# Retention scores of two heads: one full-height product on zero-padded queries, or two half-height products with a bank each

## The chip, the cores and the metric

The kernel runs on one core of a Trainium2 chip. A core has a matrix engine (TensorE, PE in the profile, with its weight loads shown apart as PEld), three engines for element-wise work (VectorE = DVE, ScalarE = ACT, GpSimd = POOL) and queues that start DMA transfers (SP among them). TensorE multiplies what lies in SBUF and writes the products to PSUM, which has eight banks of 128 rows x 512 float32 here; DVE and ACT read them from there. The metric is the device time of one execution in microseconds (us). The kernel before takes 247.51 us, the median of three runs (247.45 to 247.79).

## The reference, cut to what matters

Two layers follow each other. The first is a retention (a linear attention with decay), for 4 batches, 8 heads, 768 positions and 64 channels per head:

```python
gamma = 1.0 - 2.0 ** (-5.0 - np.arange(H))
for t in range(S):
    state = gamma * state + einsum('bhd,bhe->bhde', k[:, :, t], v[:, :, t])
    y[:, :, t] = scale * einsum('bhd,bhde->bhe', q[:, :, t], state)
```

The second layer takes the 8 x 64 channels of a position as one row of 512. It mixes the rows with the real part of a Fourier transform over positions and channels, adds that to the input (u), normalises u, and adds a two-layer network: `u + relu(norm(u) @ w_ch1) @ w_ch2`, with 2048 hidden channels.

## The kernel before, in words

**The retention in chunks.** The 768 positions are six chunks of 128 (NCH). Within a chunk the output is (scores x mask) x values; what came before the chunk enters through a 64 x 64 state per head. Two heads are worked on together, as the 64 + 64 rows of one 128-row tile. Four such pairs make a batch (PAIR_ORDER gives their order). For each pair of batches two to four (b = 1, 2, 3 in the code) these units are emitted:

- `cast_unit` brings q, k and v to 16 bits on POOL, with the decay of the keys folded in.
- `t_unit` transposes q and k, on TensorE for b = 1 (tiles `tq`, L550, copied out by ACT at L556 and L561) and by DMA for b = 2 and 3. The transposed keys `kT` hold head one in rows 0 to 63 and head two in rows 64 to 127. The transposed queries `qTz` exist twice: `qT[:, 0]` has head one in its upper rows and zeros below, `qT[:, 1]` zeros above and head two below.
- `a_unit` makes the scores. It has three parts of two chunks each. Because of the zeros, one product of all 128 rows with the 256 columns of both padded copies (L594) gives the scores of head one in the first 128 columns and of head two in the other 128. Two chunks fill one bank, `wkA`. One DVE instruction (L597) multiplies this bank of 512 columns by the causal mask with its decay, `maskp`, and writes `atm` in 16 bits.
- `kv_unit` makes the state: products `wkK` (L613), then a chain of DVE instructions (L623), with a copy by ACT (L619) at its head.
- `y_unit` makes the output: state products (L644), then the products of `atm` with the values (L648), in a bank per head, `wkY`. ACT evicts them (L656). It reads the padded queries too, in full height.

Batch one has units of its own (L458 for its scores, evicted at L465), in which the heads are taken from the half rows of an unpadded tile.

**The banks.** `wkA`, `wkK`, `wkY`, `tq` and the products of the Fourier part share the pool `ps_g` of five banks. The network's products `psh` and `psc` have the pool `ps_pm` of three.

**The network.** `h_unit` (L930) makes one block of 128 hidden channels by four products of 384 columns; ACT (L934) or DVE (L936) applies relu. `ch_unit` (L973) makes 128 output rows by sixteen products of 512 columns, in four units; DVE scales them and adds u (L977).

**The order.** The network of batch b and the retention and Fourier part of batch b + 1 run together. `attn_steps` makes six lists of units per batch (steps); each list, and the network's list, is a stream with a start and an end on a scale of batches. `emit` places the units of a stream evenly between these, merges all streams by place, and emits them in that order. For b = 2 and 3 the start and end of a step follow from the number of units in the steps. The framework then orders each engine's instructions. TensorE takes its instructions in order: when a product waits for a bank, all behind it wait. Loads of the batch after next wait for the last score product of pair 1 (`a_of`). `filler` (L145) are products on zeros that bridge idle time while batch one starts.

Of the kernel before, what the change touches and what calls it, by code (L numbers as in the profile page):

```python
# [12 lines left out]
ALU = mybir.AluOpType  # L13
f32 = mybir.dt.float32
# [4 lines left out]
P = 128  # L19
B, H, S, D = 4, 8, 768, 64  # L20
# [9 lines left out]
PAIR_ORDER = [0, 1, 3, 2]  # L30
# [7 lines left out]
def kernel(  # L38
# [9 lines left out]
    nc = tc.nc  # L48
# [3 lines left out]
    def pool(name, bufs, **kw):  # L52
        return ctx.enter_context(tc.tile_pool(name=name, bufs=bufs, **kw))
# [16 lines left out]
    ps_g = pool("ps_g", 5, space=PSUM)  # L70
# [13 lines left out]
    maskp = const.tile([P, NHP, 2, P], f32, tag="maskp")  # L84
# [36 lines left out]
    def held(unit):  # L121
        def run():
            ins = tc.nc.cur_bb.bb.instructions
            n0 = len(ins)
            unit()
            for n in range(n0, len(ins)):
                m = n - 1
                while m >= 0 and ins[m].engine != ins[n].engine:
                    m -= 1
                if m >= 0:  # L130
                    tc.add_manual_dep(ins[n], ins[m].name,
                                      mybir.DependencyInfo(mybir.DependencyClass.NoSync,
                                                           mybir.DependencyReason.DATA),
                                      reason="casts in turn")
        return run
# [450 lines left out]
    def a_unit(b, i, part):  # L586
        def run():
            st = at[b, i]
            if part == 0:
                st["atm"] = ap_.tile([P, NCH, 2, P], f16, tag="atm", name="atm")  # L590
            wk = ps_g.tile([P, 2, 2, P], f32, tag="g", name="wkA")
            for c2 in range(2):
                c = 2 * part + c2
                mm = nc.tensor.matmul(wk[:, c2], st["kT"][:, c, :], st["qT"][:, :, c, :],  # L594
                                      start=True, stop=True)
            a_of[b, i] = mm
            nc.vector.tensor_tensor(  # L597
                out=st["atm"][:, 2 * part:2 * part + 2], in0=wk,
                in1=maskp[:, PAIR_ORDER[i]].unsqueeze(1).to_broadcast([P, 2, 2, P]),
                op=ALU.mult)  # L600
        return run

    def kv_unit(b, i):
        def run():
            st = at[b, i]
            hp = PAIR_ORDER[i]
            kd, v16 = kd_of[b, i], v16_of[b, i]
            s16 = sp.tile([P, NCH - 1, P], f16, tag="s16", name="s16")
            st["s16"] = s16
            for c0, n in ((0, 3), (3, 2)):  # L610
                wk = ps_g.tile([P, 3, P], f32, tag="g", name="wkK", padded_shape=[P, 4, P])
                for c in range(c0, c0 + n):
                    nc.tensor.matmul(wk[:, c - c0, :], kd[:, c].rearrange("p a b -> p (a b)"),  # L613
                                     v16[:, c].rearrange("p a b -> p (a b)"),
                                     start=True, stop=True)
                for c in range(c0, c0 + n):
                    if c == 0:
                        if ON_ACT["kv"][min(b, 2)]:
                            nc.scalar.copy(s16[:, 0], wk[:, 0])  # L619
                        else:  # L620
                            nc.vector.tensor_copy(s16[:, 0], wk[:, 0])
                    else:
                        nc.vector.scalar_tensor_tensor(out=s16[:, c], in0=s16[:, c - 1],  # L623
                                                       scalar=gk2[:, hp:hp + 1],
                                                       in1=wk[:, c - c0],
                                                       op0=ALU.mult, op1=ALU.add)
        return run

    def y_unit(b, i):
        def run():  # L630
            st = at.pop((b, i))
            hp = PAIR_ORDER[i]
            v16, s16, atm, qT = v16_of[b, i], st["s16"], st["atm"], st["qT"]
            ypool, ytag = (ps_pm, "pm") if b == 0 else (ps_g, "g")
            yk = [ypool.tile([P, NCH, D], f32, tag=ytag, name="wkY", padded_shape=[P, 8, D])
                  for _ in range(2)]
            for c in range(1, NCH):
                for h2 in range(2):
                    sl = slice(64 * h2, 64 * h2 + 64)
                    if b == 0:  # L640
                        lhsT, rhs = qT[sl, c, :], s16[sl, c - 1, sl]
                    else:
                        lhsT, rhs = qT[:, h2, c, :], s16[:, c - 1, sl]
                    nc.tensor.matmul(yk[h2][:, c, :], lhsT, rhs,  # L644
                                     start=(c == 1), stop=False, skip_group_check=True)
            for h2 in range(2):
                for c in range(NCH):
                    nc.tensor.matmul(yk[h2][:, c, :], atm[:, c, h2, :], v16[:, c, h2, :],  # L648
                                     start=False, stop=(c == NCH - 1), skip_group_check=True)
                h = 2 * hp + h2  # L650
                x = xts[b % 2]
                if h < 4:
                    dst = x[:, :, 0, 64 * h + 1:64 * h + 65]
                else:
                    dst = x[:, :, 1, 513 - 64 * h:449 - 64 * h:-1]
                nc.scalar.activation(dst, yk[h2], AF.Copy, bias=0.0, scale=gq8[:, h:h + 1])  # L656
        return run
# [4 lines left out]
    def fold_s(b, lo, hi, s0, s1):  # L662
        def run():
            x = xts[b % 2]
            if b not in fd:
                fd[b] = dict(
                    ab=fp.tile([P, 2, 3, 2, XW], f16, tag="xab", name="xab"),
                    eo=fp.tile([P, 2, 2, 3, 256], f16, tag="eo", name="eo"),
                    g=gp.tile([P, 4, KN], f16, tag="g16", name="g16"),
                    gr=gp.tile([P, 4, 384], f16, tag="g16r", name="g16r"))  # L670
            ab = fd[b]["ab"]
            for a, op in ((0, ALU.add), (1, ALU.subtract)):
                nc.vector.tensor_tensor(out=ab[:, a, :, s0:s1, lo:hi],
                                        in0=x[:, 0:3, s0:s1, lo:hi],
                                        in1=x[:, 3:6, s0:s1, lo:hi], op=op)
        return run

    def fold_d(b, cb, es=(0, 1)):
        def run():
            ab, eo = fd[b]["ab"], fd[b]["eo"]  # L680
            i0 = 2 + 128 * cb
            for e in es:
                nc.vector.tensor_tensor(out=eo[:, e, :, :, 128 * cb:128 * cb + 128],
                                        in0=ab[:, :, :, 0, i0:i0 + 128],
                                        in1=ab[:, :, :, 1, i0:i0 + 128],
                                        op=(ALU.add, ALU.subtract)[e])
        return run
# [60 lines left out]
    def g0_unit(b, parts=(0, 1, 2)):  # L748
        def run():
            for part in parts:  # L750
                (g0_a, g0_b, g0_c)[part](b)
        return run
# [247 lines left out]
    def attn_steps(b):  # L1000
        steps = []
        for step in range(6):
            un = []
            if step < 4:
                un.append(held(cast_unit(b, step)))
            i = step - 1
            if 0 <= i < 4:
                un.append(kv_unit(b, i))
            i = step - 2
            if 0 <= i < 4:  # L1010
                un.append(y_unit(b, i))
                if i == 2:
                    un += [fold_s(b, 0, 130, 0, 2), fold_d(b, 0)]
                    if b < FB:
                        un += [g0_unit(b), s1_unit(b, 0, 0), s1_unit(b, 1, 0)]
            if step < 4:
                un.append(t_unit(b, step))
            i = step - 1
            if 0 <= i < 4:
                if b == 0:  # L1020
                    un += [a0_unit(b, i, 0), a0_unit(b, i, 1)]
                else:
                    un += [a_unit(b, i, part) for part in range(3)]
            if step == 5:
                un += [fold_s(b, 130, 258, 0, 2), fold_d(b, 1)]
                if b >= FB:
                    un += [g0_unit(b), fold_e(b, 0), fold_e(b, 1)]
            steps.append(un)
        return steps
# [148 lines left out]
```

## Time and profile before

| | |
|---|---|
| median time | 247.51 us |
| span of the profiled execution | 246.0 us |
| score products of batches two to four, L594 | 72, 128 x 256, first at 57.7 us, last at 175.2 us |
| their masked evictions, L597 | 36, 685 ns each, 23.9 us busy |
| score products of batch one, L458 | 48, half height, 128 columns |
| their evictions, L465 | 16, 548 ns each |
| network, L930 and L973 | 448 and 400 products |

How to read it: a busy time is the union of the engine's instructions; matmuls overlap each other, and an L594 product is shown with a length of 273 ns though the next one starts after 109 ns. So a cost on TensorE is read from the starts of neighbouring products. A chain lists the work that ended last, each piece released by the one ahead of it; an engine's idle time matters only where it is on this chain.

### The profile page before, as it was taken

The page shows a single profiled execution, that of the slowest core. Times are in us where ns is not written, and L with a number is a line of the kernel's source. Part 1 is how long each engine was busy: PE and PEld are TensorE (multiplying, and loading weights), DVE is VectorE, ACT ScalarE, POOL GpSimd, SP SyncE. Part 2 cuts the span into 40 slices and gives each one's busy share as a digit, 9 for nine tenths or more (in the row PEclk, how much of TensorE's full clock was granted, in tenths as well). Part 3 has the DMA queues.
Part 4 walks back from the last instruction along what each step waited for, and adds up shares of the span by engine and source line. Part 5 has one row for each costly group of instructions (what it writes and reads, how often), then busy time and mean ns, then how long its engine had stood idle before and what let it go on. Part 6 is the DMA issues. An engine that isn't in the chain of part 4 may idle for free.

```text
span 246.0 us, 5309 instructions
## 1 busy us (share of the span) xinstructions
PE 234.4 (95%) x2024; PEld 144.4 (59%) x2024; DVE 177.5 (72%) x430; ACT 124.3 (51%) x276; POOL 81.3 (33%) x146
## 2 busy tenths in 40 slices
PE   6897899999999999999999999999999998999994
PEld 2454668956676655665567446665666455445543
DVE  8998957898788788995987648887895657424122
ACT  8798669477785445742247415732257217202500
POOL 6667600376500068690001637660003214000000
PEclk9999999999999999999999999999999999999999
DMA  8998999699999287988999589596100331121012
GB/s 174 257 260 138 200 204 206 152 250 261 275 233 214 56 171 176 190 174 149 242 266 210 119 183 181 108 138 150 58 0 3 60 133 30 38 85 43 0 45 85
DMA packets 99209, 36.39 MB, mean 148 GB/s; under 512 B 89840, under 2 KB 96240, under 8 KB 99184
## 3 DMA queue, kind: packets, MB, share of 16 engines
q1 hardware_dynamic: 94960, 31.86, 62.5%
q0 software_dynamic: 4224, 4.19, 10.5%
q8 instruction: 16, 0.26, 0.5%
q14 instruction: 9, 0.07, 0.1%
HBM read 27.26 MB, written 6.29 MB: 136 GB/s over the span
## 4 chain that ended last, share of the span: by engine, by line
PE 72%; DVE 8%; POOL 7%; ACT 4%; SPq 3%; DMA 2%; issue 2%; POOLq 0%; DVEq 0%
PE psc L973 30%; PE psh L930 23%; SPq L159 3%; PE ps L730 3%; PE psh L947 3%; PE wkA L594 3%; DMA k<-in_k_dram 2%; PE wkY L648 2%; POOL u L864 2%; POOL u L866 2%; PE wkY L644 1%; DVE bst L883 1%; PE wkK L613 1%; DVE u L834 1%; PE pq L827 1%
## 5 line engine op out<-in xcount | busy, mean ns | idle before, releaser
L973 PE MATMUL psc<-w,ht 128*128 128x512 f16 (+1 forms) x400 | 89.6, 370 | 0.1
L930 PE MATMUL psh<-unT,w 128*128 128x384 f16 x448 | 81.3, 326 | 0.6 <-ACT ht L934 0.6
L973 PEld LDWEIGHTS <-ht 128*128 128x128 f16 x400 | 38.1, 98 | 35.5 <-issue 0.3
L930 PEld LDWEIGHTS <-w 128*128 128x128 f16 x448 | 42.3, 98 | 24.9 <-issue 1.3
L934 ACT ACTIVATE ht<-psh 128x384 f16<-128x384 f32 x64 | 30.6, 488 | 39.4 <-PE psh L930 38.3
L864 POOL TENSOR_TENSOR u<-u,x 128x256 f32<-128x256 f32 x21 | 13.3, 634 | 102.3 <-DVE u L834 90.7
L977 DVE SCALAR_TENSOR_TENSOR ob<-psc,stats,u 128x512 f32<-128x512 f32 (+1 forms) x25 | 18.1, 722 | 27.4 <-PE psc L973 27.3
L936 DVE TENSOR_SCALAR ht<-psh 128x384 f16<-128x384 f32 x48 | 26.3, 551 | 8.6 <-PE psh L930 8.3
L597 DVE TENSOR_TENSOR atm<-wkA,maskp 128x512 f16<-128x512 f32 x36 | 23.9, 685 | 1.0 <-PE wkA L594 1.0
L885 ACT ACTIVATE un<-u,stats 128x512 f16<-128x512 f32 x21 | 15.1, 721 | 16.9 <-DVE stats L884 8.7
L883 DVE BATCH_NORM_STATS2 bst<-u 128x6 f32<-128x512 f32 x21 | 14.6, 694 | 9.7 <-POOL u L866 9.5
L623 DVE SCALAR_TENSOR_TENSOR s<-s,gk,wkK 128x128 f16<-128x128 f16 x48 | 16.4, 343 | 2.3 <-ACT s L619 1.4
L656 ACT ACTIVATE x<-wkY,gexp 128x384 f16<-128x384 f32 x24 | 12.8, 580 | 9.3 <-PE wkY L648 9.3
L145 PE MATMUL wps<-ht 128*128 128x512 f16 x40 | 13.3, 439 | 2.2 <-POOL ht L196 2.2
L377 POOL TENSOR_SCALAR kd<-k,gexp 128x384 f16<-128x384 f32 x24 | 13.8, 584 | 2.4 <-DMA k<-in_k_dram 2.4
L866 POOL TENSOR_TENSOR u<-u,x 128x256 f32<-128x256 f32 x21 | 13.3, 634 | 2.8 <-DVE u L837 1.5
L594 PE MATMUL wkA<-qTz,kT 128*128 128x256 f16 x72 | 13.6, 273 | 0.0
L829 ACT COPY qn<-pq 128x128 f32<-128x128 f32 x18 | 4.9, 274 | 14.1 <-PE pq L827 13.9
L947 PE MATMUL psh<-unT,w 128*128 128x128 f16 x192 | 11.5, 219 | 0.1
L947 PEld LDWEIGHTS <-w 128*128 128x128 f16 x192 | 11.0, 98 | 0.7 <-issue 0.5
L382 POOL TENSOR_SCALAR v<-v 128x768 f16<-128x768 f32 x12 | 10.0, 830 | 2.0 <-DMA v<-in_v_dram 1.9
L594 PEld LDWEIGHTS <-kT 128*128 128x128 f16 x72 | 6.9, 98 | 6.0 <-DVE s L623 0.4
(164 smaller groups left out, 318.2 us busy)
## 6 DMA issues: line engine op xcount, KB each, us to landing
q<-in_q_dram SPq DMA_DIRECT2D x16, 384.0 KB, 6.2
k<-in_k_dram SPq DMA_DIRECT2D x16, 384.0 KB, 5.6
v<-in_v_dram SPq DMA_DIRECT2D x16, 384.0 KB, 6.6
out_dram<-ob SPq DMA_DIRECT2D x23, 256.0 KB, 2.6
w<-in_moe_w_ch_dram POOLq DMA_DIRECT2D x8, 512.0 KB, 11.1
out_dram<-ob SPq DMA_DIRECT2D x2, 128.0 KB, 1.7
unT<-un SPq DMA_TRANSPOSE x15, 2.4
qTz<-q16z SPq DMA_TRANSPOSE x8, 3.8
```

The lines of the kernel that those rows point to most:

```text
L594: mm = nc.tensor.matmul(wk[:, c2], st["kT"][:, c, :], st["qT"][:, :, c, :], start=True, stop=True)
L597: nc.vector.tensor_tensor(out=st["atm"][:, 2 * part:2 * part + 2], in0=wk, in1=maskp[:, PAIR_ORDER[i]].unsqueeze(1).to_broadcast([P, 2, 2, ...
L623: nc.vector.scalar_tensor_tensor(out=s16[:, c], in0=s16[:, c - 1], scalar=gk2[:, hp:hp + 1], in1=wk[:, c - c0], op0=ALU.mult, op1=ALU.add)
L864: nc.gpsimd.tensor_tensor(out=u[:, kb, 0:256], in0=u[:, kb, 0:256], in1=x[:, kb, 0, 1:257], op=ALU.add)
L866: nc.gpsimd.tensor_tensor(out=u[:, kb, 256:512], in0=u[:, kb, 256:512], in1=x[:, kb, 1, 257:1:-1], op=ALU.add)
L883: nc.vector.bn_stats(bst, u[:, kb, :])
L930: nc.tensor.matmul(psh, w116[:, cb, fb * P:(fb + 1) * P], unT[:, cb, rt * 384:(rt + 1) * 384], start=(cb == 0), stop=(cb == 3))
L934: nc.scalar.activation(ht16[:, fb, :], psh, AF.Relu, bias=0.0, scale=-1.0)
L936: nc.vector.tensor_scalar(out=ht16[:, fb, :], in0=psh, scalar1=-1.0, scalar2=0.0, op0=ALU.mult, op1=ALU.max)
L947: mm = nc.tensor.matmul(psh[:, f], w116[:, cb, fb * P:(fb + 1) * P], unT[:, cb, kb * P:(kb + 1) * P], start=(cb == 0), stop=(cb == 3))
L973: nc.tensor.matmul(psc[:, c0:c1], ht16[:, fb, rb3 * P:(rb3 + 1) * P], w216[:, fb, c0:c1], start=(fb == 0), stop=(fb == NFB - 1))
L977: nc.vector.scalar_tensor_tensor(out=ob[:, c0:c1], in0=psc[:, c0:c1], scalar=lb[b]["st"][:, rb, 3:4], in1=lb[b]["u"][:, rb, c0:c1], op0=AL ...
```

## The change

The scores of batches two to four are made as batch one makes them. `a_unit` gets two parts of three chunks in place of three of two. In each chunk, head one is a product of rows 0 to 63 of keys and queries alone, head two of rows 64 to 127. The heads write to a bank each (384 of its 512 columns). There are 144 products of 128 columns in place of 72 of 256, which do not multiply the zeros, and the two of a chunk stand in different row halves of the array. Each bank is evicted by its own DVE instruction of 384 columns, 48 in place of 36. The padded queries stay, since `y_unit` reads them. The aim is to use both halves of the array for two heads at once.

```diff
     def a_unit(b, i, part):
         def run():
             st = at[b, i]
+            hp = PAIR_ORDER[i]
             if part == 0:
                 st["atm"] = ap_.tile([P, NCH, 2, P], f16, tag="atm", name="atm")
-            wk = ps_g.tile([P, 2, 2, P], f32, tag="g", name="wkA")
-            for c2 in range(2):
-                c = 2 * part + c2
-                mm = nc.tensor.matmul(wk[:, c2], st["kT"][:, c, :], st["qT"][:, :, c, :],
-                                      start=True, stop=True)
+            wk = [ps_g.tile([P, 3, P], f32, tag="g", name="wkA", padded_shape=[P, 4, P])
+                  for _ in range(2)]
+            for c3 in range(3):
+                c = 3 * part + c3
+                for h2 in range(2):
+                    sl = slice(D * h2, D * h2 + D)
+                    mm = nc.tensor.matmul(wk[h2][:, c3, :], st["kT"][sl, c, :],
+                                          st["qT"][sl, h2, c, :], start=True, stop=True)
             a_of[b, i] = mm
-            nc.vector.tensor_tensor(
-                out=st["atm"][:, 2 * part:2 * part + 2], in0=wk,
-                in1=maskp[:, PAIR_ORDER[i]].unsqueeze(1).to_broadcast([P, 2, 2, P]),
-                op=ALU.mult)
+            for h2 in range(2):
+                nc.vector.tensor_tensor(
+                    out=st["atm"][:, 3 * part:3 * part + 3, h2, :], in0=wk[h2],
+                    in1=maskp[:, hp, h2].unsqueeze(1).to_broadcast([P, 3, P]), op=ALU.mult)
         return run
...
-                    un += [a_unit(b, i, part) for part in range(3)]
+                    un += [a_unit(b, i, part) for part in range(2)]
```

## The prediction

> **What bounds the kernel now.** I read three views: engine totals and the chain of the page, then a table by stretches, then the chain and the TensorE timeline around the products that change.
>
> ```profile
> PE 234.4 (95%) x2024; PEld 144.4 (59%) x2024; DVE 177.5 (72%) x430; ACT 124.3 (51%) x276; POOL 81.3 (33%) x146
> ...
> PE 72%; DVE 8%; POOL 7%; ACT 4%; SPq 3%; DMA 2%; issue 2%; POOLq 0%; DVEq 0%
> ```
>
> TensorE is busy for 95% and holds 72% of the chain that ended last. A matmul's end is modelled, though, so stretches are needed (columns: stretch, length, then busy us and instructions of PE, its weight loads, DVE, ACT, POOL).
>
> ```profile
> 57.00:80.00 23.00, 22.93 (x249) 15.63 (x247) 19.75 (x44) 16.38 (x31) 6.45 (x9) 1.00 1.19 243
> ...
> 100.00:126.00 26.00, 26.00 (x238) 16.33 (x237) 21.94 (x50) 10.77 (x25) 8.17 (x14) 1.00 1.08 194
> ...
> 150.00:178.00 28.00, 27.60 (x248) 17.14 (x247) 23.61 (x55) 11.65 (x28) 11.74 (x21) 1.00 0.63 130
> ```
>
> These are the stretches with the score products of batches two, three and four. PE has no gap in the middle one, 0.07 and 0.40 us in the others; DVE is at 84 to 86%. The chain there (start, length, engine, line):
>
> ```profile
> 106.76 0.22 PE wkA L594 x2
> 106.98 0.65 PE psh L930 x4
> 107.63 0.22 PE wkA L594 x2
> 107.85 0.65 PE psh L930 x4
> 108.50 0.22 PE wkA L594 x2
> 108.72 0.86 PE psc L973 x4
> ```
>
> The chain is TensorE's own queue, one product after another: 0.22 us for two score products, 0.109 each, with MLP products (psh, psc) on both sides. So any time that this queue gains or loses here reaches the end nearly one to one, and the question is what a group of half-height products costs *between full-height ones*. Batch one already does it (L458):
>
> ```profile
> 17.87 0.60 PE L145 MATMUL wps<-ht 128*128 128x512 f16 x2
> 18.41 0.51 PE L458 MATMUL wkA<-qTz,kT 64*128 64x128 f16 x12
> 18.85 0.39 PE L145 MATMUL wps<-ht 128*128 128x512 f16 x1
> ```
>
> Twelve half-height products, six pairs, start at 18.41; the next full-height one starts at 18.85. I also took the single starts from the trace. The two of a pair start 3 ns apart. Pair follows pair after 67, then 56, 56, 56, 56 ns. The last pair's second product is followed by the full-height one after 149 ns, not 53: 96 ns lost. The full 512-column product ahead of the group is followed by it after 312 ns, though such products otherwise follow each other after 216: again 96 ns. The first gap after the group is 226 ns, not 216. The entry into batch one's other half-height products (L520) is 126 against 29 ns behind 64-column products at 12.6 us, and 152 against 56 behind transposes at 23.1 us: 96 or 97 each time, whatever is ahead.
>
> **What the Trainium skill says.** *TensorEngine Tiling (Array Packing)*, Tiling Modes, Key Properties: "Changing tiling mode (not just tile) drains the TensorE". The trace agrees, with 96 ns on entry and 96 on exit. *TensorE: Matmul & The Clock Gate*, Part 3, The mechanism: products in different row groups overlap with about 4 ns between starts; here 3 to 4 ns. The tiling page, Gotcha 1: PSUM Pressure: different row tiles write to different banks; this is why each head now has a bank of its own. *Perfetto Trace Analysis*, Optimizing Scalar/DVE Operations: about 125 ns of overhead per DVE instruction on PSUM; the 685 and 548 ns below give 137 by extrapolation.
>
> **The change part by part.**
>
> *TensorE, removed.* 72 products of 256 columns. Per half of a pair of heads (three chunks) 3 x 109 = 327 ns, for 24 halves 7.8 us.
>
> *TensorE, added.* 144 half-height products. In the built order of instructions they stand in 22 groups of three pairs and in 4 broken groups of three products; never do two groups touch, as the MLP lies between. A whole group: entry 96, pairs 67 + 56, last pair up to the next full-height product 3 + 149, first gap behind 10: 381 ns, so 54 more than before. 22 x 54 = 1.19 us. A broken group of three products (one pair, one single): 96 + 67 + 149 + 10 = 322 ns where one and a half chunks took 164: 158 more. 4 x 158 = 0.63 us. Sum: **+1.8 us on TensorE**. The overlap alone is worth 24 x (327 - 3 x 56) = 3.8 us; twice 96 and twice about 10 ns at 26 groups, 5.5 us, eat it, and the halved pairs do the rest.
>
> *What hides some of it.* In the first step of batch two TensorE already waits: the trace has gaps of 0.17 us at 59.2 and 0.23 at 60.1, which end with ACT's copies of the transposes (0.80 us each, in the chain there). Three of the 26 groups, two of them broken, stand there. I take 0.2 of their 0.37 us as absorbed: +1.6.
>
> *DVE.* 36 masked evictions of 512 columns at 685 ns (24.7 us) become 48 of 384. The nearest row is batch one's eviction of the same shape (L465, another operation) at 548 ns: 26.3 us, +1.6 in total or +0.14 per pair of heads. Bounds: three quarters of 685, 514 ns (no change), and the longest of the L465 row, 558 ns (+2.1). DVE has 14 to 16% free in these stretches, so most of it hides beside TensorE. It is seen where the products with the values (L648) wait for the last eviction: three such waits, 0.7 us in all, now. I allow +0.2 us.
>
> *PSUM banks.* ps_g has five banks. A step of batches three and four took seven (two wkK, two wkY, three wkA); it takes eight, and a group needs two at once. Behind a group that waits stands the whole TensorE queue, MLP included. In the new order the second group of a pair follows the first by four MLP products (0.65 to 0.86 us), and its banks are those of wkK and wkY, which DVE (343 ns a step of the state) and ACT (580 ns) must have left. No wait of this kind is in the trace, so: low end 0; high end two evictions of the first group (1.1 us) less the four MLP products between (0.65), 0.45 us, where the banks do not come free earlier, in one pair of three, 4 x 0.45 = 1.8 us. I take 0: between the groups of one pair and of the next there are some 3 us of other products, in which banks come free.
>
> *At nothing:* loads of later batches wait for the last score product of pair 1, which moves by less than 0.2 us while their transfers take 6 us and are not on the chain; the fewer units per step shift some MLP products by one place, beside a queue that is full either way.
>
> Sum: 247.5 + 1.6 + 0.2 = **249.3 us**.
>
> **Rivals.**
> *A, the pairing wins.* If the drain were overlapped by weight loads, or paid on one side only, a group costs 381 - 106 = 275, 52 less than before: 24 x 52 = 1.2 us saved, 246.3 (with no drain at all 3.8, 243.7). For it: PEld is only 59% busy. Against: the 96 ns stand on both sides in every group of batch one where nothing is waited for. A reshuffled order that loses some of the waits of TensorE at 95.1 us (0.63) and 157.0 us (0.52) would end here too.
> *B, absorbed.* The single gaps of TensorE over 60 ns between 57 and 206 us sum to 3.2 us. If half of that were slack that the longer queue fills, 249.3 - 1.6 = 247.7. Against: most end with DVE or POOL work that hangs on earlier products of the same queue, so they move along with it.
> *C, banks and DVE bind.* The high ends: 249.3 + 1.8 = 251.1. For it: DVE is the second busiest engine and now evicts four times in a row, ahead of the MLP's evictions (551 ns). Against: half of the groups stand among psc products, whose bank is needed only every sixteen products (3.5 us).
>
> **How the numbers follow.** Forecast 0.62; A 0.13; B 0.12; C 0.13. The forecast has +1.8 +/- 0.7. Range: 247.6, which leaves out A and part of B, to 250.6, which leaves out half of C. Faster by over 0.2%: A, 0.13. Within: most of B, 0.11. Slower: the forecast, C and the rest of B, 0.76.
>
> **What would show it.** L598 with 144 products of 64 x 128, pairs 3 ns apart; full-height product to group some 96 ns late, and again out of it. The evictions at 530 to 570 ns, x48. The stretches of batches two to four longer by 0.4 to 0.8 us each, still with PE busy throughout, and the ends (0 to 57, 205 to the end) unchanged in length. Wrong would be: no drain beside the MLP's products (A); new gaps of TensorE ahead of L598, wkK or wkY that end with DVE or ACT (C); or old gaps that shrink by what the groups gain in length (B).

## The result, and the profile after

The changed kernel takes 251.32 us (median of 4 runs, 251.11 to 251.42), the kernel before 247.65 on the same chip: 1.0147 times as long, 95% interval 1.0133 to 1.0161, +3.7 us. The direction was as predicted, the size twice that, and outside the range (247.6 to 250.6).

The page's totals and chain:

```profile
PE 236.7 (95%) x2096; PEld 140.2 (56%) x2096; DVE 178.4 (72%) x442; ACT 124.2 (50%) x276; POOL 81.7 (33%) x146
...
PE 68%; DVE 11%; POOL 7%; ACT 4%; SPq 3%; DMA 3%; issue 2%; POOLq 0%; ACTq 0%; DVEq 0%
```

TensorE's share of the chain fell from 72 to 68%, DVE's rose from 8 to 11%. So something besides TensorE's own work has entered the path. The stretches of the prediction (length, then busy us of PE, its weight loads, DVE, ACT, POOL):

```profile
57.00:80.00 23.00, 22.85 (x270) 13.81 (x268) 19.36 (x47) 16.24 (x30) 6.47 (x9) 1.00 1.18 244
100.00:126.00 26.00, 25.61 (x254) 14.20 (x253) 21.39 (x52) 9.77 (x24) 8.90 (x15) 1.00 1.12 204
150.00:178.00 28.00, 27.03 (x252) 14.98 (x251) 23.15 (x58) 11.07 (x28) 12.33 (x21) 1.00 0.58 130
```

In batch three, where TensorE had no gap, it now has 0.39 us of gaps, and in batch four 0.97 in place of 0.40. DVE is no fuller than before in any of them.

The drains are there (TensorE, start and length):

```profile
106.38 1.46 PE L934 MATMUL psh<-unT,w 128*128 128x384 f16 x8
107.78 0.34 PE L598 MATMUL wkA<-qTz,kT 64*128 64x128 f16 x6
108.05 0.82 PE L934 MATMUL psh<-unT,w 128*128 128x384 f16 x4
108.90 0.21 PE L598 MATMUL wkA<-qTz,kT 64*128 64x128 f16 x1
109.37 0.32 PE L598 MATMUL wkA<-qTz,kT 64*128 64x128 f16 x5 [0.26 <-ACT x L660]
```

Read from the starts of single products, the group at 107.78 comes 258 ns after the last product ahead of it (162 without the switch: 96 lost); the next network product comes 149 ns after the group's last one (53 without the switch: 96 lost again), and the gap behind that is 173 ns, not 162. The group at 108.90 shows what was not foreseen: after one product it stands still for 0.47 us until ACT has evicted a `wkY` bank.

**A ledger of TensorE's queue.** I sorted the time between neighbouring starts, from the first `wkK` of batch two to the end, into three kinds. *Scores*: the score products at the spacing that they have without a wait (109 ns per 256 columns, 3 and 55 ns in a pair), the 96 ns of each switch, and excesses of under 60 ns beside them. *Waits*: elsewhere, all time beyond the usual gaps of 29, 56, 109, 162 and 216 ns (64, 128, 256, 384 and 512 columns); beside scores, excesses of over 60 ns. *Rest*: all else, with the time before that `wkK`, so that the three add up to the span.

| kernel (us of its profiled execution) | scores | waits | rest | span |
|---|---|---|---|---|
| before | 8.02 | 5.23 | 232.75 | 246.0 |
| changed | 9.66 | 7.05 | 232.72 | 249.4 |
| difference | +1.64 | +1.82 | -0.03 | +3.4 |

About half of the loss is the drains, less what the pairs gain by overlap, at the price foreseen; the other half is new waiting. (The table is of one execution of each kernel; these lie 3.4 us apart, the medians 3.7.)

**Where the new waits come from.** DVE around the largest one, near 161 us in batch four, and TensorE at the end of it:

```profile
158.73 0.55 DVE L602 TENSOR_TENSOR atm<-wkA,maskp 128x384 f16<-128x384 f32 x1
159.76 0.70 DVE L887 BATCH_NORM_STATS2 bst<-u 128x6 f32<-128x512 f32 x1 [0.49 <-POOL u L870]
160.38 0.54 DVE L602 TENSOR_TENSOR atm<-wkA,maskp 128x384 f16<-128x384 f32 x1
...
160.97 0.26 PE L652 MATMUL wkY<-v,atm 128*128 128x64 f16 x3 [0.79 <-DVE atm L602]
```

The chain of waits through this stretch (start, length, engine, what):

```profile
158.50 0.40 POOL u L868
...
159.10 0.65 POOL u L870
...
159.76 0.70 DVE bst L887
160.46 0.47 DVE atm L602
...
160.97 0.26 PE wkY L652 x3
```

The fourth eviction of pair 0 stands in DVE's order *behind* the statistics of the last Fourier row block (L887). These wait for POOL to add x to u (L868 and L870, 0.6 us each), with DVE idle for 0.49 us. The products with the values wait for the fourth eviction, and TensorE loses 0.96 us there (by the starts, as in the ledger). In the kernel before, the third and last eviction stands *ahead* of the same statistics:

```profile
156.83 0.68 DVE L597 TENSOR_TENSOR atm<-wkA,maskp 128x512 f16<-128x512 f32 x1
157.86 0.69 DVE L883 BATCH_NORM_STATS2 bst<-u 128x6 f32<-128x512 f32 x1 [0.35 <-POOL u L866]
```

The wait for POOL is there before too, but no eviction of this pair's scores stands behind it. Batch three shows the same at 106.3 us (0.28 us) and the bank wait at 109 us on top.

### The profile page after: what moved, and what is told of

Read it like the earlier page. It is cut to its first block, busy times and chain, and to the rows that moved or that the text cites. A ratio compares the mean times of both kernels' runs of the same rounds, so it can differ in the third digit from the quotient of the medians.

```text
span 249.4 us, 5468 instructions
## 1 busy us (share of the span) xinstructions
PE 236.7 (95%) x2096; PEld 140.2 (56%) x2096; DVE 178.4 (72%) x442; ACT 124.2 (50%) x276; POOL 81.7 (33%) x146
## 4 chain that ended last, share of the span: by engine, by line
PE 68%; DVE 11%; POOL 7%; ACT 4%; SPq 3%; DMA 3%; issue 2%; POOLq 0%; ACTq 0%; DVEq 0%
PE psc L977 30%; PE psh L934 20%; PE ps L734 3%; SPq L159 3%; PE psh L951 3%; DMA k<-in_k_dram 2%; PE wkA L598 2%; DVE bst L887 2%; POOL u L870 2%; POOL u L868 1%; PE wkY L652 1%; DVE atm L602 1%; DVE u L838 1%; PE tq L550 1%; PE pq L831 1%
## 5 line engine op out<-in xcount | busy, mean ns | idle before, releaser
L977 PEld LDWEIGHTS <-ht 128*128 128x128 f16 x400 | 37.3, 98 | 36.7 <-issue 0.3
L934 PEld LDWEIGHTS <-w 128*128 128x128 f16 x448 | 41.0, 98 | 26.2 <-issue 1.3
L868 POOL TENSOR_TENSOR u<-u,x 128x256 f32<-128x256 f32 x21 | 13.3, 636 | 105.8 <-DVE u L838 93.0
L889 ACT ACTIVATE un<-u,stats 128x512 f16<-128x512 f32 x21 | 15.1, 721 | 18.7 <-DVE stats L888 9.5
L602 DVE TENSOR_TENSOR atm<-wkA,maskp 128x384 f16<-128x384 f32 x48 | 24.3, 548 | 0.0
L887 DVE BATCH_NORM_STATS2 bst<-u 128x6 f32<-128x512 f32 x21 | 14.6, 694 | 10.1 <-POOL u L870 9.9
L627 DVE SCALAR_TENSOR_TENSOR s<-s,gk,wkK 128x128 f16<-128x128 f16 x48 | 16.4, 341 | 3.0 <-ACT s L623 1.7
L870 POOL TENSOR_TENSOR u<-u,x 128x256 f32<-128x256 f32 x21 | 13.3, 635 | 2.5 <-DVE u L862 1.3
L951 PEld LDWEIGHTS <-w 128*128 128x128 f16 x192 | 11.0, 98 | 0.7 <-issue 0.5
L741 ACT CAST g<-ps 128x386 f16<-128x386 f32 x14 | 7.7, 601 | 4.6 <-PE ps L734 4.6
L677 DVE TENSOR_TENSOR xab<-x 128x780 f16<-128x780 f16 (+4 forms) x18 | 8.6, 510 | 1.9 <-ACT x L660 1.9
```

The costliest lines, as they stand in the source:

```text
L602: nc.vector.tensor_tensor(out=st["atm"][:, 3 * part:3 * part + 3, h2, :], in0=wk[h2], in1=maskp[:, hp, h2].unsqueeze(1).to_broadcast([P, 3 ...
L868: nc.gpsimd.tensor_tensor(out=u[:, kb, 0:256], in0=u[:, kb, 0:256], in1=x[:, kb, 0, 1:257], op=ALU.add)
L870: nc.gpsimd.tensor_tensor(out=u[:, kb, 256:512], in0=u[:, kb, 256:512], in1=x[:, kb, 1, 257:1:-1], op=ALU.add)
L887: nc.vector.bn_stats(bst, u[:, kb, :])
L889: una = nc.scalar.activation(un, u[:, kb, :], AF.Identity, bias=stats[:, kb, 0:1], scale=-1.0)
L934: nc.tensor.matmul(psh, w116[:, cb, fb * P:(fb + 1) * P], unT[:, cb, rt * 384:(rt + 1) * 384], start=(cb == 0), stop=(cb == 3))
```

## The experiments

Theory 1: two separate costs, the drains and waits from the place in DVE's order. Rivals: 2, the waits only follow from TensorE being late through the drains; 3, DVE simply has more to do, or five banks are too few. Ratios are to the kernel before on the same chip, with 95% intervals.

| kernel | time, us | ratio | scores | waits |
|---|---|---|---|---|
| changed | 251.32 | 1.0147 (1.0133 to 1.0161) | 9.66 | 7.05 |
| E1 full height, two banks | 250.86 | 1.0127 (1.0114 to 1.0140) | 8.04 | 8.48 |
| E2 before, with switches | 253.72 | 1.0235 (1.0222 to 1.0248) | 15.57 | 3.79 |
| E3 one group, four banks | 254.18 | 1.0253 (1.0224 to 1.0282) | 8.33 | 13.08 |
| E4 early evictions | 249.47 | 1.0069 (1.0057 to 1.0081) | 9.59 | 5.36 |
| E5 full height and early | 248.57 | 1.0032 (1.0021 to 1.0044) | 8.07 | 6.07 |
| E6 before, early | 247.91 | 1.0008 (1.0002 to 1.0015) | | |
| E7 late statistics | 249.97 | 1.0091 (1.0078 to 1.0104) | 9.64 | 5.97 |
| E8 before, third eviction behind | 249.10 | 1.0057 (1.0044 to 1.0071) | 7.97 | 6.74 |
| E9 values evicted first | 250.43 | 1.0110 (1.0092 to 1.0128) | 9.62 | 6.31 |
| E10 last three pairs in one go | 248.11 | 1.0026 (1.0020 to 1.0033) | 7.33 | 6.49 |

E6 has no ledger, since its traced execution was disturbed (1353 us).

**E1.** The change without its half height.

```diff
-                    mm = nc.tensor.matmul(wk[h2][:, c3, :], st["kT"][sl, c, :],
-                                          st["qT"][sl, h2, c, :], start=True, stop=True)
+                    mm = nc.tensor.matmul(wk[h2][:, c3, :], st["kT"][:, c, :],
+                                          st["qT"][:, h2, c, :], start=True, stop=True)
```

> The changed kernel with full-height products on the padded queries (144 of 128 columns, 56 ns each), so with no change of tiling mode. Banks, evictions and the written order of TensorE and DVE are those of the changed kernel. Theory 1 (the 3.7 us are two separate costs: 1.8 of drains, and as much of new waits that come from four evictions and eight bank takings a step): the waits stay, 249.2 to 249.7 us, with TensorE waiting again about 0.9 us ahead of a wkY product near 160 us. Theory 2 (all of it is the drains, and the waits only follow from TensorE being late): 247.5 to 247.9.

250.86 us, slower than either theory said; rival 2 is out. Without one drain the kernel loses, by the ratios, 3.1 of the 3.6 us. The scores fall by 1.62 us against the changed kernel, as the prices say, and the waits rise by 1.43: TensorE comes sooner to the same places and waits there longer (0.96 us near 161, as in the changed kernel, and 0.89 near 109 in place of 0.50).

**E2.** Drains without the rest: the kernel before, with two mode changes in each group.

```diff
-            for c2 in range(2):
-                c = 2 * part + c2
-                mm = nc.tensor.matmul(wk[:, c2], st["kT"][:, c, :], st["qT"][:, :, c, :],
-                                      start=True, stop=True)
+            for h2 in range(2):
+                rows = slice(0, D) if h2 == 0 else slice(0, P)
+                for c2 in range(2):
+                    c = 2 * part + c2
+                    mm = nc.tensor.matmul(wk[:, c2, h2], st["kT"][rows, c, :],
+                                          st["qT"][rows, h2, c, :], start=True, stop=True)
```

> The kernel before with its banks and 512-column evictions; in each of the 36 groups head one is taken as two half-height products, one after the other, and head two as two full-height ones on padded queries. So each group pays one entry and one exit of the tiling mode and gains no overlap. By the prediction's prices a group costs 96 + 67 + 149 + 10 + 2 x 56 = 434 ns in place of 218, 36 x 0.216 = 7.8 us. Theory 1: 255.0 to 255.6 us. If the drains were partly hidden on the whole path: under 252. If each drain also made others wait (theory 2): over 257.

253.72 us, +5.9, between the numbers named. The scores grew by 7.55 us, the price to within 0.3; the waits shrank by 1.44. So the price of a switch holds beside the network, and part of it is paid out of old waits.

**E3.** Both parts of a pair in one unit, four banks at once.

```diff
-            wk = [ps_g.tile([P, 3, P], f32, tag="g", name="wkA", padded_shape=[P, 4, P])
-                  for _ in range(2)]
+            wk = [ps_g.tile([P, 3, P], f32, tag="g", name="wkA", padded_shape=[P, 4, P])
+                  for _ in range(4)]
...
-                    un += [a_unit(b, i, part) for part in range(2)]
+                    un += [a_unit(b, i, 0)]
```

> The changed kernel with both parts of a pair of heads in one unit: twelve half-height products in one go, four banks taken at once, four evictions behind them. Twelve mode changes each way in place of 26. Drains alone: a group of six pairs costs 549 ns against 654 before, so 246.4 us. Theory 1: four of five banks at once bring waits of the size seen in the changed kernel or more, 248.5 to 250 us. Theory 2: 246.3 to 246.8.

254.18 us, well over both. The ledger's waits are 13.1 us; some 2.9 of them are no waits but products at half the clock (last section). One wait, in front of the rest of a group, is 2.4 us long:

```profile
156.19 0.32 PE L932 MATMUL psh<-unT,w 128*128 128x384 f16 x1
158.71 0.47 PE L596 MATMUL wkA<-qTz,kT 64*128 64x128 f16 x3 [2.20 <-DVE s L625]
```

It ends with L625, which reads the state products `wkK` and so frees their bank. On DVE this instruction stands behind the statistics, which wait 1.83 us for POOL:

```profile
157.72 0.69 DVE L885 BATCH_NORM_STATS2 bst<-u 128x6 f32<-128x512 f32 x1 [1.83 <-POOL u L868]
158.33 0.33 DVE L625 SCALAR_TENSOR_TENSOR s<-s,gk,wkK 128x128 f16<-128x128 f16 x1
```

So the largest wait with four banks also goes by a place behind these statistics.

**E4.** The cure of DVE's order: for pair 0, the score units ahead of pair 1's transposes.

```diff
-                    un += [a_unit(b, i, part) for part in range(2)]
+                    parts = [a_unit(b, i, part) for part in range(2)]
+                    un = un[:-1] + parts + un[-1:] if b > 1 and i == 0 else un + parts
```

> The changed kernel; for pair 0 of batches three and four the score units are emitted ahead of the transposes of pair 1 and so ahead of the last Fourier unit, which puts all four evictions in DVE's order ahead of the statistics that wait for POOL. Theory 1 (the fourth eviction stood behind the statistics): the waits of 0.28 us near 106 and 0.96 near 161 go, 249.9 to 250.3 us. Theory 3 (DVE simply has more to do): within 0.2 us of the changed kernel, 251.1 to 251.4.

249.47 us. Half of the loss is gone, more than the two waits named, because the bank wait near 109 went with them. Around the products with the values of pair 0 in batch four, no gap is left:

```profile
158.46 0.46 PE L648 MATMUL wkY<-s,qTz 128*128 128x64 f16 x10
158.75 0.51 PE L652 MATMUL wkY<-v,atm 128*128 128x64 f16 x12
159.10 1.46 PE L934 MATMUL psh<-unT,w 128*128 128x384 f16 x8
```

The waits are back at 5.36 us (5.23 before), so what is left is the drains. A new wait of 0.45 us stands ahead of the second score group, at 154.0.

**E5.** The edits of E1 and E4 together.

> Full-height products in two banks (no mode change) and the early evictions, both edits together. It completes a square with the changed kernel (251.3), full height (250.9) and early evictions (249.5). If drains and waits lie side by side on the path, so that each hides part of the other, the drains cost their whole 1.5 us once the waits are gone: 249.5 - 1.5 = 248.0 us (247.8 to 248.3). If they add up, 250.9 - 1.9 = 249.0.

248.57 us, between the two. The drains cost 0.0020 of the time (0.5 us) in the bad order (changed less E1) and 0.0037 (0.9 us) in the good one (E4 less E5), not the whole 1.5: here too the quicker queue waits more, 6.07 against 5.36 us. The 0.8 us left over the kernel before are waits (a second group near 153.6, 0.59 us) and the 0.05 of the scores.

**E6.** The early emission in the kernel before: the same edit with `range(3)`.

> The kernel before with the same early emission (score units of pair 0 of batches three and four ahead of the transposes of pair 1). Its three evictions stand ahead of the last statistics already. If the early emission only cures what the change brought, 247.5 to 248.0 us; if it is a gain of its own, it takes away the waits of 0.52 and 0.21 us near 157: 246.9 to 247.3.

247.91 us, no gain. So E4's 1.85 us undo what the change brought and are not a gain of the edit itself.

**E7.** The other way to the same order.

```diff
-        dm = (0.12, 0.24, 0.3, 0.38) if b == 0 else (0.004, 0.140, 0.232, 0.341)
+        dm = (0.12, 0.24, 0.3, 0.38) if b == 0 else (0.004, 0.155, 0.232, 0.341)
```

> The changed kernel with the score units in their own place; the Fourier units of row blocks three to five of a batch are spread up to 0.155 in place of 0.140 of a batch, so that the last one, with its statistics, is emitted behind the second score unit. The other way to the same order on DVE. If the place behind the statistics is the cause: 249.2 to 249.8 us. If the earlier transposes or units did it: 251.0 to 251.4.

249.97 us, 0.2 above the range named for the place, but far from the one for the earlier units: most of the cure comes from the place. It is 0.5 us weaker than E4; its ledger has 0.6 us more of waits, among them 0.28 us at 158.0 ahead of a state product.

**E8.** The ill alone, in the kernel before: the third eviction of pair 0 behind the statistics (`bn_of` keeps their instruction).

```diff
+            if b > 1 and i == 0 and part == 2:
+                tc.add_manual_dep(ev.ins, bn_of[b - 1, 5].ins.name,
+                                  mybir.DependencyInfo(mybir.DependencyClass.NoSync,
+                                                       mybir.DependencyReason.DATA),
+                                  reason="behind the statistics")
```

> The kernel before, with its three banks, 512-column evictions and full-height products; only an order is imposed: the third eviction of pair 0 in batches three and four stands behind the statistics that wait for POOL. If the place in DVE's queue is the cause, this alone brings most of the changed kernel's waits: 249.0 to 249.8 us. If it takes two banks a group or four evictions: 247.6 to 248.2.

249.10 us, +1.4 us from one exchanged place in each of two batches. Otherwise the built order changed only in a few network products on TensorE and in what follows the statistics on DVE and ACT. Three banks, three evictions, full-height products, and the same picture on DVE and on TensorE:

```profile
158.30 0.70 DVE L888 BATCH_NORM_STATS2 bst<-u 128x6 f32<-128x512 f32 x1 [0.95 <-POOL u L871]
158.91 0.67 DVE L597 TENSOR_TENSOR atm<-wkA,maskp 128x512 f16<-128x512 f32 x1
```

```profile
157.68 0.40 PE L653 MATMUL wkY<-v,atm 128*128 128x64 f16 x8
157.92 0.81 PE L935 MATMUL psh<-unT,w 128*128 128x384 f16 x4
159.64 0.29 PE L653 MATMUL wkY<-v,atm 128*128 128x64 f16 x4 [0.91 <-DVE atm L597]
```

The waits rose by 1.51 us (0.64 us near 106 in place of none, 1.08 near 160 in place of 0.21), against 1.82 in the changed kernel, which has the bank wait near 109 besides.

**E9.** That bank wait. In the changed kernel ACT evicts both `wkY` banks of pair 0 of batch three behind a row normalisation (L889), which waits for a DMA transpose. Before, one of the two evictions stood ahead of it:

```profile
105.33 0.59 ACT L656 ACTIVATE x<-wkY,gexp 128x384 f16<-128x384 f32 x1 [0.67 <-PE wkY L648]
106.83 0.72 ACT L885 ACTIVATE un<-u,stats 128x512 f16<-128x512 f32 x1 [0.91 <-DMA unT<-un]
107.45 0.57 ACT L656 ACTIVATE x<-wkY,gexp 128x384 f16<-128x384 f32 x1
```

The changed kernel:

```profile
107.65 0.72 ACT L889 ACTIVATE un<-u,stats 128x512 f16<-128x512 f32 x1 [2.20 <-DMA unT<-un]
108.28 1.04 ACT L660 ACTIVATE x<-wkY,gexp 128x384 f16<-128x384 f32 x2
```

E9 moves the last normalisation of a batch into `unT_unit` and orders it behind these evictions; the essential lines:

```diff
+                if b > 0 and kb == 5:
+                    return
...
+                if (b + 1, 0) in x_of:
+                    tc.add_manual_dep(una.ins, x_of[b + 1, 0].ins.name,
...
```

> The changed kernel with one pair of ACT instructions exchanged per batch: the evictions of wkY of pair 0 (batches three and four) stand ahead of the last normalised rows (un), which wait for a DMA transpose. DVE's order is untouched, so the waits of 0.28 us near 106 and 0.96 near 161 stay. If the waits of 0.41 and 0.09 us of the second score group near 109 are for the banks that these evictions leave, they go: 250.7 to 251.0 us. If the five banks are just too few for two at a time, 251.2 to 251.4.

250.43 us, 0.9 below the changed kernel by the ratios, a little more than expected. The evictions run at 106.46 and the second group at 108.72 starts whole:

```profile
106.46 1.04 ACT L660 ACTIVATE x<-wkY,gexp 128x384 f16<-128x384 f32 x2
107.83 0.72 ACT L918 ACTIVATE un<-u,stats 128x512 f16<-128x512 f32 x1 [0.33 <-POOL v L382]
```

The waits of 0.28 us (106.2) and 0.95 us (160.3) stay. So the wait at 109 was not for want of banks: one was held by an eviction that stood behind work that it doesn't need.

**E10.** A try to beat both: `a6_unit` is E3's unit.

```diff
-                    un += [a_unit(b, i, part) for part in range(3)]
+                    parts = [a6_unit(b, i)] if b > 1 and i else [a_unit(b, i, n)
+                                                                 for n in range(3)]
+                    un += parts
```

> The kernel before for batch two and for pair 0 of batches three and four. For the other three pairs of batches three and four, twelve half-height products in one go in four banks. By the drain prices a group of n pairs of products costs 213 + 56 n ns against 109 n, so it breaks even at n = 4; these six groups have n = 6 and save 6 x 105 = 0.63 us, 247.0 us (0.25% less than before), if no wait comes with four banks at once. These pairs stand among the psc products, away from the statistics. If four of five banks bring waits there too: 247.8 to 248.5.

248.11 us, +0.26%. The scores fell by 0.69 us, as the break-even says; the waits rose by 1.26, among them 0.41 us inside the first such group, at 108.5, and 0.24 at 123.0 and 175.5 ahead of products that use the state. No version tried is faster than the kernel before.

## Why the prediction was wrong

Right, step by step: the bound and the direction; pairs 3 to 4 ns apart; 96 ns into a group and 96 out of it, 10 ns behind; 22 whole and 4 broken groups; 48 evictions of 548 ns; and 0.24 us of old waits near 59 and 60 us absorbed, where 0.2 was taken. The drains' term, +1.8 us, is +1.64 in the ledger, where the 10 ns behind the 26 groups, 0.26 us, count as waits. E2 and E10 confirm the price away from the change. The ends did not change: the first `wkK` of batch two comes at 56.76 us before and 56.74 after, and from the start of the last Fourier product to the end it is 40.9 us in both. That each batch would lose 0.4 to 0.8 us was right for batch two alone: the first products of the Fourier part behind batch two (from xg and csn) come at 82.44 in place of 81.90, the long run of psc behind batch three at 138.33 in place of 136.31, and that behind batch four at 192.30 in place of 188.87: the batches lost 0.54, 1.48 and 1.41 us.

The step that failed is the waits: "I allow +0.2 us" for the evictions and "I take 0" for the banks, where the ledger shows +1.82 us (0.26 of them the drains' own, as said). Both terms were sized by lengths (0.14 us more of evictions per pair, 3 us of other products in which banks come free), and both go by *places*. The prediction compared TensorE's written order, counted the groups in it, and left DVE's and ACT's orders unread. These orders are fixed when the kernel is built, like TensorE's: three evictions ahead of the last statistics became three ahead and one behind, and in each of batches three and four one more eviction of `wkY` fell behind a normalisation. E8 shows that the first exchange alone, made in the kernel before, costs 1.4 us, E9 that undoing the second alone gives back 0.9 (0.74 us of waits in the ledger), and E4 that undoing the first takes the second with it.

Rival C, with 251.1 us, came nearest, and named the banks; its argument against (half of the groups stand among psc products) was true and beside the point, since pair 0 stands among psh products and Fourier units. Its 0.13 was too little.

The terms do not simply add. In E1 and E5 a queue that is 1.5 to 1.6 us shorter gained 0.5 and 0.9 us, in E2 one that is 7.6 us longer lost 5.9. "What this queue gains or loses reaches the end nearly one to one" holds only while no other engine ends the waits, which rival B named with a chance of 0.12. Open is what E4's and E5's second groups wait for, 0.45 and 0.59 us near 154: ACT's normalisation (L889) and the state on DVE (L627) end there within 0.01 us of each other, and no kernel separated the two. In E7 a group at 154.9 waits 0.43 us where the trace names the state alone.

## What to carry to other kernels

A tiling mode is paid per group, at entry and at exit: with 213 ns a group, and 56 in place of 109 ns per chunk, half-height pairs break even at four chunks in a row and gain from five, and here groups have three. When an edit changes how many instructions an in-order engine gets, compare the written order of *every* engine, and look at what stands directly ahead of each moved instruction and what that one waits for; one place behind a wait for POOL, in two batches, cost more (1.4 us) than the half height did (0.5 to 0.9). A saving on the bounding queue is worth its full size only up to the next wait that another engine ends.

## What the runs showed of the hardware that was not expected

In the wait of 2.4 us in E3, 2.2 us after the start of the last product ahead of it, the granted TensorE clock fell to half, and it came back 6.8 us later (the columns are those of the stretches above, with the clock behind POOL):

```profile
150.00:158.00 8.00, 6.52 (x55) 4.17 (x54) 5.49 (x13) 3.73 (x12) 5.32 (x9) 1.00 0.77 186
158.00:165.00 7.00, 6.29 (x27) 3.09 (x27) 4.99 (x14) 2.97 (x6) 5.07 (x9) 0.53 0.36 72
```

For about 6 us products of 384 columns started 320 ns apart in place of 162. The traced execution took 255.57 us. Of the six executions of E3, the two with the highest mean clock (1.000 and 0.998) took 252.9, the other three (0.992 and 0.993) 254.2 to 254.6. So the fall costs up to 2.7 us, and without it E3 is still 5 us slower than the kernel before. The waits of up to 1.1 us that TensorE has after batch one in the other traces were not followed by such a stretch; how long a wait has to be is not shown.
